# Halves of a tile's product alternate with scores and with the slot steps of the tile before, in the order written for TensorE

## The chip, the cores and the metric

The kernel runs on one NeuronCore of a Trainium2 chip. Five engines work side by side, each in the order of its own queue: PE (TensorE: matmul, with PEld loading its weights), DVE (VectorE), ACT (ScalarE), POOL (GpSimd), and SP, which here only issues DMAs. They wait for one another through semaphores. PE writes to PSUM alone; DVE and ACT read it from there. The metric is the device time of one launch in microseconds, lower is better.

## The reference, cut to what matters

Block-sparse attention is followed by a soft mixture of experts. The attention has 4 batches, 8 heads, 768 positions and 64 elements per head, in blocks of 32 positions. A block of queries sees its own block and both neighbours, the first and the last block, and three sampled blocks; the first and the last query block see everything.

```python
scores = scale * np.matmul(q, k.transpose(0, 1, 3, 2))
scores = np.where(mask, scores, -1000000000.0)
attn = softmax(scores)                       # rows, + 1e-9 below
x = (attn @ v).transpose(0, 2, 1, 3).reshape(3072, 512)

logits = x @ phi                             # 3072 x 32
d = exp(logits - logits.max(0)); d /= d.sum(0) + 1e-9
slot_input = d.T @ x                         # 32 slots of 512
slot_out[e] = np.maximum(slot_input[e] @ w1[e], 0) @ w2[e]   # 8 experts, 4 slots each
c = softmax(logits)                          # over the 32 slots
out = c @ slot_out
```

All of it is float32.

## The kernel before, in words

**Units and tiles.** A batch has 26 units: 4 dense ones (the first and last query block, two head halves r, two of them j) and 22 sparse ones, for 11 pairs of query blocks (g) and two head halves (r = 0, 1). Two pairs make one tile x of 128 rows and 512 columns; pair 0 and the dense units make the tile t = 0, and five further tiles (t = 1 to 5) follow, so 24 tiles in all, 20 of them of four sparse units. Scores of a pair come in one go for r = 0 and r = 1 (L286), so every second period has a group of them. One half of a tile's product, `av_half` (L351), multiplies the probabilities of one r with the values: fixed blocks first (L360), then neighbours and sampled blocks (L378). It accumulates in `avt`, a PSUM buffer of four banks, in the first 65 columns of each. `av_out` (L333) divides by the sums (L336, L337, L339) and writes x. Both halves use the same columns. `av_dense` (L342) does the same for dense units.

**The steps from a tile to slot input**, `moe_front` (L384), in their order: e1 transposes x into PSUM (L392), DVE copies it to xT; e2 multiplies by phi (L437) into columns 128 to 255 of `avt`'s first bank, and ACT copies that to lp; e3 sums the four parts in both layouts (L444, L445), and `top` takes the running maximum (L427, L430); e3b is the exponential dT with its sum, the correction factor, and the copy of the logits to lst, all on ACT (L452 to L457); e4 transposes dT on PE (L461), DVE copies it to d and updates ssum (L465); e5 multiplies d with x (L476), DVE adds it to sacc (L479). The last tile takes other steps for the first three.

**The order.** On PE and DVE the instructions keep the order in which the code emits them; ACT, POOL and SP are ordered by the framework. The main loop goes over periods n, one unit each. A period emits: staging of keys (POOL L194, L199 and ACT L203, five units ahead) and values (POOL L214, two ahead); the scores of unit n + 2 (`do_qk`); what the list X1 holds for n, PE's part; the transpose of unit n's probabilities (`do_tr`, DVE L324); the DVE parts of X1; the row maxima and exponentials of the new unit (`do_soft`, DVE L302, ACT L305); then the list X2, PE's parts and after them DVE's. A step that returns a function leaves its evacuation to that function; e2, e4 and e5 emit theirs at once. `at(n, off, f)` puts f in X1 (even) or X2 (odd) of period n + 1 + off // 2.

Buffers that bear on it: three PSUM tiles for scores (tag s), one shared by e1, e4 and e5 (tag pt), four staged key tiles, eight value tiles, five of transposed probabilities, two of x, one each of xT, lp, dT and d. The framework orders accesses of different engines to `avt`, as to every buffer.

After the last unit come the last tile, the combine weights, and the experts' two products over weights that are partly loaded during the attention.

Of the kernel before, what the change touches and what calls it, by code (L numbers as in the profile page):

```python
# [21 lines left out]
P = 128  # L22
NP = 4
DM = H * D
NS = 32
# [15 lines left out]
KSTEP, VSTEP, EARLY = 5, 2, 4  # L41
KEARLY = 4

EOFF = [2, 3, 5, 6, 7, 8]

CS = 2
CW = DM // CS
# [16 lines left out]
def attn_moe_kernel(ctx, tc, qT, kT, vtab, sampled, phi, w1, w2, out):  # L64
# [224 lines left out]
    def do_soft(u):  # L289
        nm = pw.tile([P, 2], F32, tag="nm", name="nm", bufs=3)  # L290
        if u.dense:
            for n in range(2):
                DVE.tensor_reduce(out=nm[:, n:n + 1], in_=u.s[n], axis=AX.X, op=ALU.max, negate=True)
            nb = pw.tile([P, 1], F32, tag="nb1", name="nb1", bufs=3)
            DVE.tensor_tensor(out=nb, in0=nm[:, 0:1], in1=nm[:, 1:2], op=ALU.min)
            DVE.tensor_scalar(out=nb, in0=nb, scalar1=SCALE, scalar2=None, op0=ALU.mult)  # L296
            u.p = [pw.tile([P, 384], F32, tag="p", name="pd", bufs=PB) for _ in range(2)]
            for n in range(2):
                ACT.activation(out=u.p[n], in_=u.s[n], func=AF.Exp,  # L299
                               bias=nb, scale=SCALE)  # L300
        else:
            DVE.tensor_reduce(out=nm, in_=u.s, axis=AX.X, op=ALU.max, negate=True)  # L302
            u.p = pw.tile([P, 2, 256], F32, tag="p", name="p", bufs=PB)
            for hf in range(2):
                ACT.activation(out=u.p[:, hf, :], in_=u.s[:, hf, :], func=AF.Exp,  # L305
                               bias=nm[:, hf:hf + 1], scale=1.0)
# [8 lines left out]
    def do_tr(u):  # L315
        if u.dense:
            if u.j == 0:
                ptn[0] += 1
            u.pt = ptd[ptn[0] % NPTD]
            for n in range(2):  # L320
                DVE.transpose(out=u.pt[:, 12 * n:12 * n + 12, u.j, :], in_=u.p[n])
        else:
            u.pt = pw.tile([P, 8, 2, BLK], F32, tag="ptt", name="ptt", bufs=PTB)
            DVE.transpose(out=u.pt.rearrange("p k j q -> p j k q"), in_=u.p.rearrange("p j (k q) -> p j k q", k=8))  # L324
# [59 lines left out]
    def moe_front(b, t):  # L384
# [55 lines left out]
            evac(st["lp"], ps, "A")  # L440

        def e3():
            ps = avt[:, 1, 128:2 * P + NS]
            PE.matmul(ps[:, 0:P], lhsT=sel4, rhs=st["lp"], start=True, stop=True)  # L444
            PE.matmul(ps[:, P:P + NS], lhsT=st["lp"], rhs=sel4[:, 0:NS], start=True, stop=True)  # L445
            top(ps, ps[:, P:P + NS])
# [24 lines left out]
                DVE.reciprocal(out=ssum, in_=ssum)  # L471

        def e5():
            ps = psA.tile([P, P], F32, tag="pt", bufs=1, name="ms")
            for c in range(4):
                PE.matmul(ps[32 * c:32 * c + 32, :], lhsT=st["d"], rhs=x[:, c * P:(c + 1) * P],  # L476
                          start=True, stop=True)
            if "al" in st:
                DVE.scalar_tensor_tensor(out=sacc, in0=sacc, scalar=st["al"], in1=ps,  # L479
                                         op0=ALU.mult, op1=ALU.add)  # L480
            else:
                DVE.tensor_copy(out=sacc, in_=ps)
# [13 lines left out]
    def c_soft(g):  # L496
        l = lst[:, 4 * g:4 * g + 4]
        cm = pw.tile([P, 4], F32, tag="cm", name="cm")
        DVE.tensor_reduce(out=cm, in_=l, axis=AX.X, op=ALU.max)
        DVE.tensor_tensor(out=l, in0=l, in1=bc(cm, 4), op=ALU.subtract)  # L500
        ACT.activation(out=l, in_=l, func=AF.Exp)

    def c_norm(g):
        l = lst[:, 4 * g:4 * g + 4]
        cm = pw.tile([P, 4], F32, tag="cm", name="cm")
        DVE.tensor_reduce(out=cm, in_=l, axis=AX.X, op=ALU.add)
        DVE.tensor_scalar(out=cm, in0=cm, scalar1=EPS, scalar2=None, op0=ALU.add)
        DVE.reciprocal(out=cm, in_=cm)
        DVE.tensor_tensor(out=l, in0=l, in1=bc(cm, 4), op=ALU.mult)
# [16 lines left out]
        evac(cT[g], bank, eng)  # L526

    npre = [0]
    X1, X2 = {}, {}
    N = len(units)  # L530
    bytile, both = {}, {}
    qk = [0]
# [21 lines left out]
    def run(d, n):  # L554
        return [f for f in [f() for f in d.pop(n, [])] if f]

    for j, g in enumerate((0, 1, 2, 5)):
        X1.setdefault(N - 12 + 2 * j, []).append(lambda g=g: lambda: c_soft(g))
        X1.setdefault(N - 11 + 2 * j, []).append(lambda g=g: lambda: c_norm(g))

    def at(n, off, f):
        (X1, X2)[off % 2].setdefault(n + 1 + off // 2, []).append(f)

    vn = [0]
    for n in range(-3, N):
        if n >= 0:
            pump_k(n + KSTEP)
        while vn[0] < min(N, n + VSTEP + 1):
            u = units[vn[0]]
            if not u.dense:  # L570
                u.vst = stage_v(u.b, u.i)
            vn[0] += 1
        new = []
        while qk[0] < min(N, n + 3 + (n >= N - EARLY)):
            do_qk(units[qk[0]])
            new.append(units[qk[0]])
            qk[0] += 1
        later = run(X1, n)
        if n >= 0:
            u = units[n]  # L580
            do_tr(u)
        for f in later:
            f()
        for v in new:
            do_soft(v)
        if n >= 0:
            t = None
            if u.dense:
                if u.j == 1:
                    at(n, 0, lambda u=u: av_dense(u))  # L590
                    t = 0 if u.r == 1 else None
            else:
                tt = (u.g + 1) // 2
                bytile.setdefault((u.b, tt, u.r), []).append(u)
                if u.g % 2 == 0:
                    go = lambda b=u.b, t=tt, us=bytile[u.b, tt, u.r], r=u.r: av_half(b, t, us, r)
                    if n == N - 1:
                        last = go
                    elif n == N - 2:
                        at(n, 0, go)  # L600
                    elif u.r == 0:
                        at(n + 1, 0, go)
                    else:
                        at(n, 1, go)
                        t = tt
            if t is not None:
                if t == 0:
                    both[u.b] = both.get(u.b, 0) + 1
                if t > 0 or both[u.b] == 2:
                    fr = {}  # L610
                    for j in range(6):
                        def go(b=u.b, t=t, j=j, fr=fr):
                            if j == 0:
                                fr["f"] = moe_front(b, t)
                            return fr["f"][j]()
                        at(n, EOFF[j], go)
        for f in run(X2, n):
            f()

        while npre[0] < min(NPRE, NPRE * (n - W0) // (N - W1 - W0)):  # L620
            load_w(npre[0], wpre)
            npre[0] += 1
# [3 lines left out]

    rem = []
    for n in range(N, N + 14):
        rem += X1.pop(n, []) + X2.pop(n, [])

    def one():
        if rem:
# [282 lines left out]
```

## Time and profile before

| What | Value |
|---|---|
| median of 3 runs | 608.24 us |
| lowest, highest | 605.45, 613.77 us |
| profiled execution, its own time | 611.44 us |
| its span, first to last instruction | 609.7 us |
| mean granted TensorE clock | 0.636 |
| busy: PE, PEld | 449.6, 270.5 us |
| busy: DVE, ACT, POOL | 254.6, 186.3, 127.3 us |
| the experts' first product starts | 553.1 us |

In the timeline a row begins with its start and its length in us, the engine, the line, the operation, out<-in by the program's names, the shapes and the count of merged instructions; a bracket at the end is the idle time before it and what ended it ("issue": nothing that the profile shows). In the list of waits a row is the waiting engine and line, the releaser, the total in us, the times and the longest. In the rows of windows the columns are the stretch, its length, the busy time and count of PE, PEld, DVE, ACT and POOL, the granted clock, the DMA share and GB/s. The clock row of the page has one digit for each fortieth of the span, in tenths of full speed.

### The profile page before, as it was taken

How to read it: one execution, taken by the hardware profiler on the slowest of the kernel's cores; microseconds unless marked ns; L12 is line 12 of the kernel's file. 1: busy time of each engine (PE TensorE's matmuls, PEld its weight loads, DVE VectorE, ACT ScalarE, POOL GpSimd, SP SyncE). 2: the span in 40 equal slices, each digit the busy share in tenths (PEclk: the TensorE clock that was granted, in tenths of full speed). 3: DMA queues.
4: the chain of work that ended last, by engine and by line, in shares of the span. 5: the costliest groups of instructions: out<-in, count | busy, mean ns of one | idle time of the engine just before them, and what ended most of it. 6: DMA issues, size and time to landing. Idle time of an engine off the chain costs nothing.

```text
span 609.7 us, 28462 instructions
## 1 busy us (share of the span) xinstructions
PE 449.6 (74%) x12629; PEld 270.5 (44%) x12629; DVE 254.6 (42%) x677; ACT 186.3 (31%) x629; POOL 127.3 (21%) x391
## 2 busy tenths in 40 slices
PE   5775477668877676778966776679777765789992
PEld 1353344445355454444454444433545433563551
DVE  3444154335454433443553453354453364523132
ACT  3343144133125224321324341332242342112042
POOL 2421033312221221422101232312112132102000
PEclk9957655665576656555586556665775665557997
DMA  8677600300300003003000003003000021039997
GB/s 306 238 235 267 236 21 19 109 20 12 114 19 26 15 13 122 22 4 121 11 20 21 20 18 110 22 11 105 13 19 13 21 70 47 5 125 400 407 383 242
DMA packets 26510, 60.99 MB, mean 100 GB/s; under 512 B 2705, under 2 KB 15122, under 8 KB 26386
## 3 DMA queue, kind: packets, MB, share of 16 engines
q1 hardware_dynamic: 26386, 59.16, 27.8%
q8 instruction: 99, 1.62, 1.1%
q14 instruction: 25, 0.20, 0.1%
HBM read 52.86 MB, written 6.29 MB: 97 GB/s over the span
## 4 chain that ended last, share of the span: by engine, by line
PE 65%; DVE 13%; issue 12%; ACT 6%; ACTq 2%; DMA 1%; SPq 0%; DVEq 0%
PE avt L378 15%; PE s L286 11%; PE avt L360 10%; PE sd L275 7%; PE avt L347 5%; DVE x L339 3%; PE pf L726 3%; DVE xT L312 3%; PE avt L437 2%; PE pso L734 2%; PE ms L476 2%; PE mxt L392 2%; ACT kst L203 2%; ACT p L305 2%; DVE rs L337 1%
## 5 line engine op out<-in xcount | busy, mean ns | idle before, releaser
L305 ACT ACTIVATE p<-s,nm 128x256 f32<-128x256 f32 x176 | 73.3, 469 | 139.5 <-DVE nm L302 134.4
L214 POOL COPY vrs<-vtile 128x130 f32 x264 | 68.0, 295 | 227.9 <-PE avt L378 203.0
L378 PE MATMUL avt<-vrs,ptt 32*32 32x65 f32 x4224 | 80.0, 289 | 29.9 <-issue 29.9
L286 PE MATMUL s<-kst,qc 64*32 64x256 f32 x1408 | 89.1, 608 | 10.1 <-ACT p L305 7.9
L336 DVE TENSOR_SCALAR rs<-avt 128x4 f32<-128x4 f32 (+1 forms) x56 | 9.0, 161 | 186.5 <-PE avt L378 161.2
L360 PE MATMUL avt<-vtile,ptt 32*64 32x65 f32 x2816 | 61.9, 312 | 31.7 <-DVE x L339 22.7
L378 PEld LDWEIGHTS avt<-vrs,ptt 32*32 32x32 f32 x4224 | 66.9, 129 | 36.9 <-issue 34.5
L199 POOL TENSOR_SCALAR kst<-ktile 128x384 f32<-128x384 f32 x88 | 44.6, 510 | 144.5 <-PE s L286 143.4
L203 ACT ACTIVATE kst<-ktile 128x128 f32 x264 | 63.3, 300 | 36.8 <-PE s L286 23.8
L360 PEld LDWEIGHTS avt<-vtile,ptt 32*64 32x64 f32 x2816 | 51.7, 199 | 49.6 <-DVE x L339 27.3
L302 DVE TENSOR_REDUCE nm<-s 128x2 f32<-128x512 f32 x88 | 59.5, 678 | 30.0 <-PE s L286 29.8
L324 DVE STREAM_TRANSPOSE ptt<-p 128x512 f32<-128x512 f32 x88 | 61.8, 702 | 0.1
L275 PE MATMUL sd<-ktile,qd 64*32 64x384 f32 x256 | 48.1, 826 | 9.5 <-DMA ktile<-in_kT_dram 5.5
L286 PEld LDWEIGHTS s<-kst,qc 64*32 64x32 f32 x1408 | 30.0, 150 | 41.2 <-issue 21.2
L310 ACT COPY lp<-avt 128x128 f32<-128x128 f32 x23 | 6.1, 265 | 135.3 <-PE avt L437 135.3
L347 PE MATMUL avt<-vtile,ptd 32*64 32x65 f32 x1536 | 32.5, 251 | 4.5 <-issue 4.5
L347 PEld LDWEIGHTS avt<-vtile,ptd 32*64 32x64 f32 x1536 | 30.8, 166 | 9.9 <-issue 6.3
L392 PE MATMUL mxt<-ident,x 128*128 128x128 f32 x92 | 28.9, 421 | 7.9 <-DVE x L339 7.9
L437 PE MATMUL avt<-xT,phis 128*32 128x128 f32 x184 | 14.8, 404 | 24.6 <-DVE xT L312 22.8
L299 ACT ACTIVATE pd<-sd,nb 128x384 f32<-128x384 f32 x32 | 16.8, 576 | 45.5 <-DVE nb L296 26.9
L378 PE MATMUL avt<-vtile,ptt 32*32 32x65 f32 x1280 | 24.9, 299 | 2.9 <-issue 2.6
L339 DVE TENSOR_TENSOR x<-avt,rs 128x256 f32<-128x256 f32 (+1 forms) x56 | 23.7, 424 | 1.9
(106 smaller groups left out, 385.5 us busy)
## 6 DMA issues: line engine op xcount, KB each, us to landing
w<-in_w_dram SPq DMA_DIRECT2D x52, 512.0 KB, 9.4
ktile<-in_kT_dram SPq DMA_DIRECT2D x16, 384.0 KB, 5.7
kw<-in_w_dram SPq DMA_DIRECT2D x12, 512.0 KB, 5.6
qc<-in_qT_dram SPq DMA_DIRECT2D x44, 128.0 KB, 2.0
out_dram<-ob SPq DMA_DIRECT2D x20, 256.0 KB, 3.9
vtile<-in_vtab_dram SPq DMA_DIRECT2D x4, 845.0 KB, 5.0
vtile<-in_vtab_dram SPq DMA_DIRECT2D x4, 780.0 KB, 7.3
qd<-in_qT_dram SPq DMA_DIRECT2D x4, 128.0 KB, 2.1
```

The lines of the kernel that those rows point to most:

```text
L199: POOL.tensor_scalar(out=st[:, :, w:w + 96], in0=kv[:, :, (i - 1) * BLK:(i + 2) * BLK], scalar1=SCALE, scalar2=1.0, op0=ALU.mult, op1=ALU. ...
L203: ACT.activation(out=st[:, :, o:o + BLK], in_=kv[:, :, ds(vals[j] * BLK, BLK)], func=AF.Copy, scale=SCALE)
L214: POOL.tensor_copy(out=st[:, j:j + 1, :], in_=vf[:, ds(vals[j], 1), :])
L275: PE.matmul(u.s[n][32 * p:32 * p + 32, :], lhsT=qd[s_, p, u.j, :], rhs=kt[s_, p, 384 * n:384 * (n + 1)], start=True, stop=True)
L286: PE.matmul(u.pair_of[r].s[32 * p:32 * p + 32, j, :], lhsT=q[s_, p, j, :], rhs=kst_[s_, p, :], start=True, stop=True)
L302: DVE.tensor_reduce(out=nm, in_=u.s, axis=AX.X, op=ALU.max, negate=True)
L305: ACT.activation(out=u.p[:, hf, :], in_=u.s[:, hf, :], func=AF.Exp, bias=nm[:, hf:hf + 1], scale=1.0)
L324: DVE.transpose(out=u.pt.rearrange("p k j q -> p j k q"), in_=u.p.rearrange("p j (k q) -> p j k q", k=8))
L339: DVE.tensor_tensor(out=x[lo:hi, r], in0=a[:, :, 0:D], in1=rs[lo:hi].unsqueeze(2).to_broadcast([hi - lo, NP, D]), op=ALU.mult)
L347: PE.matmul(avt[64:128, p, 0:D1], lhsT=u.pt[s_, k].rearrange("p j q -> p (j q)"), rhs=vt[s_, k, u.r, :], start=(k == 0), stop=(k == NB - 1))
L360: PE.matmul(avt[o:o + 64, p, 0:D1], lhsT=u.pt[s_, c].rearrange("p j q -> p (j q)"), rhs=vt[s_, k, r, :], start=(n == 0), stop=False)
L378: PE.matmul(avt[o:o + 32, p, 0:D1], lhsT=u.pt[s_, c, j, :], rhs=v_, start=False, stop=(n == NR))
```

## The change

The two lists become three, addressed by period: X[0] and X[1] are emitted before the scores, X[2] at the end of the period. The first half of a tile's product goes into X[0] of the period after its last unit (before: two periods after), the second half into X[0] of the next one, the dense products into X[0] as well. e1 to e5 get the periods and lists of `EOFF`, counted from the tile's last unit, or of `EOFFL` for the fifth unit from the end. New units with r = 1, whose scores came a period earlier, get their maxima and exponentials before the lists' DVE parts. e3 moves from `avt` to the buffer pt, and e5 from pt to the fourth bank of `avt`.

For a tile whose last unit is n this gives, on PE: period n: first half, then e2 and e3 of the tile before; n + 1: second half, e4 of the tile before, a group of scores; n + 2: e5 of the tile before, e1; n + 3: a group of scores.

```diff
-EOFF = [2, 3, 5, 6, 7, 8]
+EOFF = [(2, 2), (4, 1), (4, 2), (4, 2), (5, 1), (6, 2)]
+EOFFL = [(2, 2), (3, 1), (3, 2), (3, 2), (4, 1), (5, 0)]
...
         def e3():
-            ps = avt[:, 1, 128:2 * P + NS]
+            ps = psA.tile([P, P + NS], F32, tag="pt", bufs=1, name="mlt")
...
         def e5():
-            ps = psA.tile([P, P], F32, tag="pt", bufs=1, name="ms")
+            ps = avt[:, 3, 128:2 * P]
...
-    X1, X2 = {}, {}
+    X = [{}, {}, {}]
...
-    def at(n, off, f):
-        (X1, X2)[off % 2].setdefault(n + 1 + off // 2, []).append(f)
+    def at(n, k, f):
+        X[k].setdefault(n, []).append(f)
...
         new = []
+        later = run(X[0], n) + run(X[1], n)
         while qk[0] < min(N, n + 3 + (n >= N - EARLY)):
             do_qk(units[qk[0]])
             new.append(units[qk[0]])
             qk[0] += 1
-        later = run(X1, n)
         if n >= 0:
             u = units[n]
             do_tr(u)
+        early = [v for v in new if not v.dense and v.r == 1]
+        for v in early:
+            do_soft(v)
         for f in later:
             f()
         for v in new:
-            do_soft(v)
+            if v not in early:
+                do_soft(v)
...
-                    at(n, 0, lambda u=u: av_dense(u))
+                    at(n + 1, 0, lambda u=u: av_dense(u))
...
-                    elif n == N - 2:
-                        at(n, 0, go)
-                    elif u.r == 0:
+                    else:
                         at(n + 1, 0, go)
-                    else:
-                        at(n, 1, go)
-                        t = tt
+                        t = tt if u.r else None
...
-                if t > 0 or both[u.b] == 2:
+                if n < N - 1 and (t > 0 or both[u.b] == 2):
...
-                        at(n, EOFF[j], go)
-        for f in run(X2, n):
+                        d, k = (EOFFL if n == N - 5 else EOFF)[j]
+                        at(n + d, k, go)
+        for f in run(X[2], n):
             f()
...
-        rem += X1.pop(n, []) + X2.pop(n, [])
+        rem += X[0].pop(n, []) + X[1].pop(n, []) + X[2].pop(n, [])
```

More of the change, by code (lines that the diff above doesn't have):

```diff
@@ L557, in attn_moe_kernel @@
     for j, g in enumerate((0, 1, 2, 5)):
-        X1.setdefault(N - 12 + 2 * j, []).append(lambda g=g: lambda: c_soft(g))
-        X1.setdefault(N - 11 + 2 * j, []).append(lambda g=g: lambda: c_norm(g))
-    def at(n, off, f):
-        (X1, X2)[off % 2].setdefault(n + 1 + off // 2, []).append(f)
+        X[1].setdefault(N - 12 + 2 * j, []).append(lambda g=g: lambda: c_soft(g))
+        X[1].setdefault(N - 11 + 2 * j, []).append(lambda g=g: lambda: c_norm(g))
+    def at(n, k, f):
+        X[k].setdefault(n, []).append(f)
     vn = [0]
```

## The prediction, made before the change was run

> **What bounds the kernel now.** I read the page first, then the waits, then the timeline of one tile, engine by engine.
>
> ```profile
> PE 449.6 (74%) x12629; PEld 270.5 (44%) x12629; DVE 254.6 (42%) x677; ACT 186.3 (31%) x629; POOL 127.3 (21%) x391
> PEclk9957655665576656555586556665775665557997
> PE 65%; DVE 13%; issue 12%; ACT 6%; ACTq 2%; DMA 1%; SPq 0%; DVEq 0%
> ```
>
> PE is the bound, but not alone: it is busy 74% of the span, and a quarter of the chain that ended last (13 + 12%) is DVE or PE's own issue. From the third slice to the 35th the clock row reads mostly 5 to 7. The waits name what PE stands for, in us, times and longest:
>
> ```profile
> PE avt L378 <- issue: 32.6, 22, 5.6
> PE avt L437 <- DVE xT L312: 22.8, 23, 1.6
> PE avt L360 <- DVE x L339: 22.7, 23, 1.4
> PE md L461 <- ACT dT L452: 21.0, 15, 2.8
> PE s L286 <- ACT p L305: 7.9, 3, 2.6
> PE mxt L392 <- DVE x L339: 7.9, 20, 0.6
> ACT sp L310 <- DVE sp L312: 7.4, 2, 5.5
> ```
>
> Four of them are one pattern, once per tile: PE issues a step and the next thing in its written order needs the evacuation of that step. One tile of the steady part, PE's rows:
>
> ```profile
> 338.20 0.66 PE L437 MATMUL avt<-xT,phis 128*32 128x128 f32 x8 [0.78 <-DVE xT L312]
> 338.78 1.96 PE L286 MATMUL s<-kst,qc 64*32 64x256 f32 x32
> 340.67 0.80 PE L444 MATMUL avt<-lp,sel 128*128 128x128 f32 x2
> 341.26 0.47 PE L445 MATMUL avt<-sel,lp 128*128 128x32 f32 x2
> 343.03 0.31 PE L461 MATMUL md<-ident,dT 32*128 32x32 f32 x1 [1.30 <-ACT dT L452]
> 343.27 1.96 PE L286 MATMUL s<-kst,qc 64*32 64x256 f32 x32
> 345.16 0.65 PE L476 MATMUL ms<-x,d 128*32 128x128 f32 x8
> 345.75 1.30 PE L360 MATMUL avt<-vtile,ptt 32*64 32x65 f32 x64
> ...
> 349.39 0.91 PE L378 MATMUL avt<-vrs,ptt 32*32 32x65 f32 x40 [0.94 <-issue]
> 351.30 1.30 PE L360 MATMUL avt<-vtile,ptt 32*64 32x65 f32 x64 [1.00 <-DVE x L339]
> ...
> 355.89 0.69 PE L392 MATMUL mxt<-ident,x 128*128 128x128 f32 x2 [0.30 <-DVE x L339]
> 357.36 0.66 PE L437 MATMUL avt<-xT,phis 128*32 128x128 f32 x8 [0.78 <-DVE xT L312]
> ```
>
> From 338.20 to 357.36 a tile takes 19.16 us, of which 1.30 + 0.94 + 1.00 + 0.30 + 0.78 = 4.32 are waits and 14.84 PE's own work. The first half of the tile's product (r0) runs from 345.75 to 350.30, 3.6 us without its 0.94; the second (r1) starts at 351.30 on the same PSUM columns. e1 to e5 are the rows of L392, L437, L444 with L445, L461 and L476, the steps that turn a finished tile x into slot input.
>
> **The change, part by part.** No work is added or removed; in this sum every matmul keeps its price. PE's new order of a tile, read from the lists: r0, e2, e3, r1, e4, scores, e5, e1, scores, where e2 to e5 belong to the tile before, and e1 to this one. The other rows that I need:
>
> ```profile
> 338.96 0.27 ACT L310 COPY lp<-avt 128x128 f32<-128x128 f32 x1 [6.84 <-PE avt L437]
> 341.20 0.71 ACT L203 ACTIVATE kst<-ktile 128x128 f32 x3 [0.44 <-PE s L286]
> 341.81 0.82 ACT L305 ACTIVATE p<-s,nm 128x256 f32<-128x256 f32 x2
> 343.45 0.17 DVE L312 COPY d<-md 128x32 f32<-128x32 f32 x1
> 346.15 0.70 DVE L324 STREAM_TRANSPOSE ptt<-p 128x512 f32<-128x512 f32 x1
> 350.41 0.16 DVE L336 TENSOR_SCALAR rs<-avt 128x4 f32<-128x4 f32 x1 [3.56 <-PE avt L378]
> 350.82 0.42 DVE L339 TENSOR_TENSOR x<-avt,rs 128x256 f32<-128x256 f32 x1
> 351.16 0.68 DVE L302 TENSOR_REDUCE nm<-s 128x2 f32<-128x512 f32 x1
> ```
>
> *r1 no longer follows r0.* r0's normalisation runs from 350.41 to 351.24, 0.83 us, and r1 started 0.06 later. Now e2 (0.66) and e3 (340.67 to 341.73, 1.06) lie between. The buffer named avt has its columns for e2 beside those of r0, and the last wait above (of the experts' part) shows that neighbours in one PSUM buffer are ordered although they share no column, reads included: ACT's copy of one half of sp stood 7.4 us for DVE's copy of the other half. So DVE's normalisation waits for e2 and for lp: about 0.66 + 0.43 later, done 0.66 + 0.43 + 0.83 = 1.92 us after r0. r1 comes 0.66 + 0.43 + 1.06 = 2.15 us after r0. The wait goes: 22.7 us. The cover is 0.2 us thin; without it r1 pays that remainder, not the old 1.00.
>
> The Trainium skill, "PSUM — Partial Sum Buffer", section "PSUM bank collisions raise a hardware error", speaks against putting e2 there: two engines may not access one bank and quadrant together, reads included, so something must order them. The trace agrees with the order (the 7.4 us); by the rule or by the rows the sum is the same only while the 0.2 us hold, and 0.2 x 20 = 4 us worse if they don't (an estimate).
>
> *e1 moves away from r1, e2 away from e1.* e1 now has e4 and 1.96 us of scores behind r1, and the normalisation needs 0.83: the 7.9 us go. e2 has scores and r0 in front, 5 us, where it stood 0.78 us for the xT copy: the 22.8 us go. *e4 behind r1:* dT has r1, 3.6 us like r0, as cover instead of 1.30 us of standing: the 21.0 us go. In all 22.7 + 7.9 + 22.8 + 21.0 = 74.4 us.
>
> *e3 directly behind e2* is the new wait: no scores lie between. From the end of e2 at 338.86: lp starts 0.10 later, takes 0.27, and PE starts 0.06 after what it waits for: 0.43 us. Below that it cannot be; above, if two exponentials stand before lp in ACT's queue, 0.43 + 0.82 = 1.25. I take 0.43, since those exponentials' scores lie a whole r0 earlier: 0.43 x 23 = 9.9 us, at most 29.
>
> *e4's copy d now stands ahead of DVE's transpose of the period.* It waits for e4, thus for r1, and queued behind it are ssum, a transpose, r1's normalisation and the row maximum. From the end of e4: 0.1 to the start of d, which takes 0.17, ssum (one column) about as long, so 0.4; the transpose to 1.1, the normalisation to 2.0 us. PE has 1.9 us of scores; e5, now in avt, must wait for the normalisation's read: 0.1 us, 2 us in 20 tiles. No one else waits: the half that needs the transpose is a period away.
>
> *Scores close to scores.* Between the two groups lie only e5 and e1, 0.65 and two pairs like that at 355.89, together some 1.3, where both halves lay. There are three score tiles, so the second group needs the exponentials of the first one's first unit: maximum at 2.0 to 2.7 us, exponentials to 3.6. PE is there at 1.9 + 0.1 + 0.65 + 1.3 = 3.95. It fits by 0.35. Not if ACT runs both groups of staging copies first (2 x 0.71): then 1.42 - 0.35 = 1.07 us, 21 us in 20 tiles. The second copy starts 0.44 us after what it waits for, and ends before the maximum does, so I take 0. A gain (the 7.9 us of scores behind exponentials) isn't counted either; those are three places around the dense units.
>
> POOL's and SP's transfers keep their periods; value slots come free earlier. The last tiles use a shorter list, and I cost them at nothing: the product tail behind them is unchanged.
>
> *Issue stays.* In this stretch PE stands without a named releaser:
>
> ```profile
> 369.21 0.30 PE L378 MATMUL avt<-vrs,ptt 32*32 32x65 f32 x2 [1.48 <-issue]
> 370.50 1.30 PE L360 MATMUL avt<-vtile,ptt 32*64 32x65 f32 x64 [1.00 <-DVE x L339]
> 371.73 0.52 PE L378 MATMUL avt<-vtile,ptt 32*32 32x65 f32 x32
> 372.06 0.75 PE L378 MATMUL avt<-vrs,ptt 32*32 32x65 f32 x30
> 374.34 1.22 PE L378 MATMUL avt<-vrs,ptt 32*32 32x65 f32 x66 [1.52 <-issue]
> ```
>
> Between the two stops lie 2 + 64 + 32 + 30 = 128 matmuls. That looks like blocks of 128 matmuls with their weight loads, where the next block arrives late: 5.13 us here. One half has 64 + 32 + 30 + 66 = 192 matmuls, so a block that falls inside it still runs out, and one that spans both halves didn't. I keep the 32.6 us.
>
> Sum: the profiled execution took 611.4 us; 611.4 - 74.4 + 9.9 + 2 = 548.9. The median of the runs is 608.2, 0.5% lower, so **546**.
>
> **Rivals.** *The clock rises.* At the granted clock of 1.00 the same steps are shorter:
>
> ```profile
> 316.50:325.50 9.00, 3.97 (x89) 2.20 (x81) 6.52 (x15) 5.46 (x20) 0.99 (x3) 1.00 0.05 15
> 338.20:347.00 8.80, 7.50 (x154) 3.96 (x155) 4.69 (x11) 6.01 (x23) 2.10 (x5) 0.50 0.11 32
> 319.94 1.09 PE L286 MATMUL s<-kst,qc 64*32 64x256 f32 x32
> ```
>
> Scores take 1.09 us instead of 1.96 (the column before the last two is the clock): 1.74 us a tile. The digits of the clock row over the tiles average about 0.6, and (0.6 - 0.5) / 0.5 is a fifth of the time at full clock. If PE without its gaps got it for three fifths: 0.4 x 20 x 1.74 = 14 us, and some 20 with the other steps: 526. For it: r0 after scores and e2 behind are 6 us without a gap. Against: 338.20 to 341.73 was gapless too, at 0.50. Chance 0.22. The Trainium skill, "TensorE: Matmul & The Clock Gate", Part 1, says that the clock is halved by default and freed by one busy window of about 3.4 us; the two values agree with the rows, the gapless 3.5 us at 0.50 only if the window's phase missed them.
>
> *The covers are too thin.* Scores wait 1.07 us (21 us), lp stands behind the exponentials (another 19): 548.9 + 40 = 589, on the median's scale 586. For it: margins of 0.35 and 0.2 us, and ACT's order isn't written by hand. Against: ACT is idle 69% of the span. Chance 0.20.
>
> *Instruction blocks become the bound, and the kernel is slower.* Two halves, two groups of scores of 32 and 25 matmuls in e1 to e5 make 473 a tile, 3.7 blocks. At 5.13 us each it would take 19.0, as long as now: 608, no change, chance 0.07. It decides at 19.16 / 3.7 = 5.2 us; at 5.5, as behind longer transfers (the 5.6 us stop), 20.4 us a tile and 608 + 25 = 633. For it: stops of 32.6 us already. Against: 22 stops, 1.5 us on the average, in 24 tiles, and steps of few matmuls between the halves give a block time to arrive. Chance 0.06. The forecast itself, 536 to 562, has 0.45.
>
> **How the numbers follow.** The range reaches from the clock case to the thin covers: 524 to 590. Outside lie the two cases of the blocks and the edges. Two percent, about what a measurement of this kernel can tell from no change, is 596 to 620: faster 0.45 + 0.22 + 0.20 = 0.87, same 0.07, slower 0.06.
>
> **What would show it.** Right: the waits of L437 on xT, L360 on x, L461 on dT and L392 on x are nearly gone from PE; L444 waits about 0.4 us for lp 23 times; a steady tile takes 16.3 us; issue keeps about 33 us. Wrong: scores (L286) wait for exponentials in every tile, e5 for the normalisation by more than 0.5 us, or r1 still waits for x; a granted clock above 0.70 means that the gain has a second source; issue above 60 us means the blocks.

## The result, and the profile after

The changed kernel takes **538.68 us** (median of four runs, 535.25 to 543.37), the kernel before 608.52 in the same comparison: a ratio of 0.883, with a 95% interval of 0.873 to 0.892. The forecast was 546, in a range of 524 to 590. The profiled execution took 535.25 us, its span is 533.5 us and its mean granted clock 0.734.

The page of the changed kernel, the rows that answer to the first fence of the prediction, with the row of the queue that brings most of the instructions (packets, MB, share of 16 engines):

```profile
PE 416.5 (78%) x12629; PEld 266.3 (50%) x12629; DVE 250.2 (47%) x677; ACT 187.0 (35%) x629; POOL 125.9 (24%) x391
PEclk9957576769577667775687777685877656589996
q8 instruction: 99, 1.62, 1.2%
```

PE does the same 12629 matmuls in 33 us less, and the clock row now reads mostly 5 to 8. Rows of the list of its waits (lines from the change on are two higher than before, further down a few more):

```profile
PE avt L380 <- issue: 44.0, 27, 4.3
PE avt L478 <- DVE x L341: 8.1, 7, 1.6
PE mlt L446 <- ACT lp L312: 7.3, 17, 0.5
PE avt L349 <- DVE sacc L481: 6.6, 3, 2.2
PE avt L362 <- issue: 6.1, 4, 3.7
PE s L288 <- ACT p L307: 4.0, 6, 1.1
PE avt L362 <- DVE ptt L326: 2.7, 7, 0.9
PE avt L349 <- DVE ptd L323: 2.6, 2, 1.3
PE avt L362 <- DVE sacc L481: 2.4, 5, 0.7
PE avt L362 <- DVE x L341: 1.6, 7, 0.2
PE avt L439 <- DVE xT L314: 0.8, 1, 0.8
```

Of the four waits of the kernel before, 74.4 us, r1's for x (L362) has 1.6 us left and e2's for xT (L439) 0.8; e1's for x and e4's for dT are not in the list any more. The largest row is now a stop with no named releaser. A tile of the steady part in the timeline, PE's rows:

```profile
304.51 1.96 PE L288 MATMUL s<-kst,qc 64*32 64x256 f32 x32
306.40 0.65 PE L478 MATMUL avt<-x,d 128*32 128x128 f32 x8
...
312.32 1.04 PE L380 MATMUL avt<-vrs,ptt 32*32 32x65 f32 x80 [0.80 <-issue]
313.28 0.43 PE L439 MATMUL avt<-xT,phis 128*32 128x128 f32 x8
314.15 0.49 PE L446 MATMUL mlt<-lp,sel 128*128 128x128 f32 x2 [0.44 <-ACT lp L312]
...
315.01 1.76 PE L362 MATMUL avt<-vtile,ptt 32*64 32x65 f32 x64 [0.24 <-DVE x L341]
...
319.53 0.52 PE L380 MATMUL avt<-vrs,ptt 32*32 32x65 f32 x28 [1.15 <-issue]
319.99 0.31 PE L463 MATMUL md<-ident,dT 32*128 32x32 f32 x1
320.23 1.96 PE L288 MATMUL s<-kst,qc 64*32 64x256 f32 x32
```

From scores to scores 15.72 us, where the tile of the prediction took 19.16 and the forecast for a steady tile was 16.3. The tiles of the changed kernel differ more than those before: counted from e2 to e2, without the stretches of the dense units and the last tile, they take 12.9 to 19.8 us, before 18.6 to 22.4.

The balance, from the page (busy) and from the whole list of PE's waits (rows with "issue" as stops, all others as named waits; some 12 us of gaps too short for the list are in neither):

| PE, us | before | after | difference |
|---|---|---|---|
| busy, the same matmuls | 449.6 | 416.5 | -33.1 |
| named waits | 101.6 | 46.7 | -54.9 |
| stops without a named cause | 46.7 | 57.3 | +10.6 |
| gaps in neither | 11.8 | 13.0 | +1.2 |
| span | 609.7 | 533.5 | -76.2 |

So three questions went to the chip: which part of the change removes which wait, where the 33 us of shorter matmuls come from, and what the stops are. My theory was that the waits' removal pays twice, once itself and once by the clock, and that the stops are blocks of 128 matmuls that arrive late, together with their weight loads. The rivals: one single piece of the change brings it all; the clock rises for another reason than the closed gaps; the stops belong to places in the work.

All runs in one table. The medians of before were 608.8, 611.3 and 610.2 us in the three comparisons that the other rows come from; ratios are to these. The last four columns are of the one profiled execution. r0_early has no interval, since three of its four runs, the profiled one among them, lie 1.6 to 1.9% above its fastest.

| Kernel | median, us | ratio, 95% interval | named waits | stops | PE busy | clock |
|---|---|---|---|---|---|---|
| before | 608.5 | | 101.6 | 46.7 | 449.6 | 0.636 |
| r0_early | 585.1 | 0.96, no interval | 89.4 | 36.1 | 446.1 | 0.664 |
| e2_near | 565.6 | 0.924 (0.920 to 0.929) | 66.1 | 50.6 | 440.9 | 0.661 |
| together | 562.9 | 0.924 (0.917 to 0.930) | 71.7 | 48.1 | 430.1 | 0.701 |
| r0_early_pt | 552.4 | 0.905 (0.898 to 0.912) | 63.6 | 45.0 | 431.8 | 0.693 |
| opt | 549.3 | 0.900 (0.896 to 0.904) | 52.2 | 49.5 | 434.0 | 0.706 |
| split_r0 | 544.2 | 0.893 (0.887 to 0.899) | 58.2 | 44.9 | 423.6 | 0.730 |
| shift | 540.2 | one run | 43.3 | 55.0 | 427.6 | 0.728 |
| after | 538.7 | 0.883 (0.873 to 0.892) | 46.7 | 57.3 | 416.5 | 0.734 |
| tr_first | 534.6 | 0.880 (0.875 to 0.884) | 46.8 | 62.2 | 402.2 | 0.774 |
| opt3 | 526.8 | 0.864 (0.859 to 0.870) | 49.6 | 44.9 | 418.5 | 0.706 |
| fill | 613.1 | 1.006 (1.002 to 1.010) | 68.3 | 52.7 | 481.1 | 0.658 |
| fill2 | 614.8 | 1.007 (1.004 to 1.011) | 64.9 | 59.9 | 475.4 | 0.713 |

### The profile page after: what moved, and what is told of

Same layout as the page of the kernel before. It is cut to its first block, busy times and chain, and to the rows that moved or that the text cites. A ratio compares the mean times of both kernels' runs of the same rounds, so it can differ in the third digit from the quotient of the medians.

```text
span 533.5 us, 28450 instructions
## 1 busy us (share of the span) xinstructions
PE 416.5 (78%) x12629; PEld 266.3 (50%) x12629; DVE 250.2 (47%) x677; ACT 187.0 (35%) x629; POOL 125.9 (24%) x391
## 4 chain that ended last, share of the span: by engine, by line
PE 61%; DVE 13%; issue 13%; DMA 5%; ACT 4%; ACTq 1%; SPq 0%; DVEq 0%
PE avt L380 15%; PE s L288 11%; PE avt L362 10%; PE avt L349 7%; PE sd L277 7%; DMA w<-in_w_dram 4%; DVE nm L304 3%; PE pf L730 3%; DVE ptt L326 2%; PE mlt L446 2%; DVE ptd L323 2%; PE avt L439 2%; ACT p L307 2%; PE mxt L394 2%; DVE x L341 1%
## 5 line engine op out<-in xcount | busy, mean ns | idle before, releaser
L380 PE MATMUL avt<-vrs,ptt 32*32 32x65 f32 x4224 | 75.8, 271 | 43.7 <-issue 43.6
L380 PEld LDWEIGHTS avt<-vrs,ptt 32*32 32x32 f32 x4224 | 63.5, 122 | 48.5 <-issue 46.6
L288 PE MATMUL s<-kst,qc 64*32 64x256 f32 x1408 | 81.0, 511 | 7.4 <-ACT p L307 4.0
L362 PE MATMUL avt<-vtile,ptt 32*64 32x65 f32 x2816 | 59.9, 278 | 13.2 <-issue 6.1
L362 PEld LDWEIGHTS avt<-vtile,ptt 32*64 32x64 f32 x2816 | 49.1, 171 | 34.4 <-issue 10.7
L338 DVE TENSOR_SCALAR rs<-avt 128x4 f32<-128x4 f32 (+1 forms) x56 | 8.4, 150 | 90.5 <-ACT lp L312 59.0
L314 DVE COPY d<-md 128x32 f32<-128x32 f32 x23 | 4.4, 191 | 97.2 <-PE md L463 97.2
L288 PEld LDWEIGHTS s<-kst,qc 64*32 64x32 f32 x1408 | 30.0, 132 | 36.7 <-issue 17.9
L349 PE MATMUL avt<-vtile,ptd 32*64 32x65 f32 x1536 | 37.9, 279 | 11.8 <-DVE sacc L481 6.6
L277 PE MATMUL sd<-ktile,qd 64*32 64x384 f32 x256 | 41.7, 734 | 5.9 <-DMA ktile<-in_kT_dram 5.2
L349 PEld LDWEIGHTS avt<-vtile,ptd 32*64 32x64 f32 x1536 | 36.4, 192 | 14.9 <-DVE sacc L481 7.4
L301 ACT ACTIVATE pd<-sd,nb 128x384 f32<-128x384 f32 x32 | 16.8, 576 | 52.8 <-DVE nb L298 50.6
L295 DVE TENSOR_REDUCE nm<-sd 128x1 f32<-128x384 f32 x32 | 17.1, 548 | 16.8 <-PE sd L277 16.7
L394 PE MATMUL mxt<-ident,x 128*128 128x128 f32 x92 | 23.2, 401 | 0.0
L380 PE MATMUL avt<-vtile,ptt 32*32 32x65 f32 x1280 | 22.4, 269 | 0.4 <-issue 0.4
```

Of the source, the lines that this page charges most:

```text
L277: PE.matmul(u.s[n][32 * p:32 * p + 32, :], lhsT=qd[s_, p, u.j, :], rhs=kt[s_, p, 384 * n:384 * (n + 1)], start=True, stop=True)
L288: PE.matmul(u.pair_of[r].s[32 * p:32 * p + 32, j, :], lhsT=q[s_, p, j, :], rhs=kst_[s_, p, :], start=True, stop=True)
L349: PE.matmul(avt[64:128, p, 0:D1], lhsT=u.pt[s_, k].rearrange("p j q -> p (j q)"), rhs=vt[s_, k, u.r, :], start=(k == 0), stop=(k == NB - 1))
L362: PE.matmul(avt[o:o + 64, p, 0:D1], lhsT=u.pt[s_, c].rearrange("p j q -> p (j q)"), rhs=vt[s_, k, r, :], start=(n == 0), stop=False)
L380: PE.matmul(avt[o:o + 32, p, 0:D1], lhsT=u.pt[s_, c, j, :], rhs=v_, start=False, stop=(n == NR))
L394: PE.transpose(ps[:, c, :], x[:, c * P:(c + 1) * P], ident)
```

## The experiments

### Parts of the change, one at a time

**r0_early**: the kernel before with the first half of a product one period earlier, so that it no longer stands directly ahead of the second.

```diff
-                        at(n + 1, 0, go)
+                        at(n, 0, go)
```

> The kernel before, with the first half of each product one period earlier and nothing else; e3 stays in avt. Theory (accesses to one buffer are ordered even between different columns): r1 no longer waits for x (22.7 us gone) and e4 no longer for dT (21.0 us gone), but r0 now writes the bank that e3b still reads and waits in their place for the copy of lst, about 1.5 us in 20 tiles, 31 us: net 13 us, 595 us. Rival (only shared columns matter): no such wait, 565 us or less.

Measured: 585.1 us, the four runs between 575 and 586, 10 below the theory's 595. Rows of the waits of r0_early:

```profile
PE avt L360 <- ACT lst L457: 27.3, 17, 1.8
PE avt L437 <- DVE xT L312: 22.8, 23, 1.7
PE mxt L392 <- DVE x L339: 9.9, 20, 0.7
```

Separating the halves takes away r1's wait for x and e4's for dT (together 43.7 us), and a new one of 27.3 takes most of it back: a half waits until ACT has copied the logits to lst. e3 still writes the buffer avt there, beside the columns of the halves. This is the ordering of neighbours in one PSUM buffer, on which the prediction counted for e2, at its full price. The named waits fall by 12.2 us, as the theory said (13); the rest of the gain is mostly stops, which fall by 10.6 and of which it said nothing.

**r0_early_pt**: the same, and e3 writes the buffer pt, as in the change.

```diff
-            ps = avt[:, 1, 128:2 * P + NS]
+            ps = psA.tile([P, P + NS], F32, tag="pt", bufs=1, name="mlt")
```

> The same, with e3 moved from avt to the buffer pt as in the change. Theory: both waits go and nothing takes their place, 608 - 44 = 565 us; with the clock's share (the changed kernel's PE is busy 33 us less, with 74 us of waits removed) about 20 us more, 545 us. Rival (the spread of e1 to e5 is what counts): little gain, 590 us or more.

Measured: 552.4 us, between the theory's 565 without the clock's share and 545 with it. Rows of the waits of r0_early_pt:

```profile
PE avt L437 <- DVE xT L312: 22.7, 23, 1.6
PE mxt L392 <- DVE x L339: 10.7, 20, 0.7
```

The wait for lst is gone, the other two stand much as before (22.7 and 10.7). These two edits, one step in time and one other buffer, bring 56 of the 70 us (608.8 to 552.4); the rest of the change brings the rest, which no run here splits up further.

**together**: the changed kernel with the two halves directly behind one another again.

```diff
+                    if u.r == 0 and n < N - 2:
+                        go = lambda go=go: go()()
...
-                        at(n + 1, 0, go)
+                        at(n + (2 if u.r == 0 and n < N - 2 else 1), 0, go)
```

> The changed kernel, with the first half moved back to stand directly before the second. Theory: r1 waits 1.0 us for x again in 20 tiles, and with the gap some full clock is lost: 538.7 + 20 = 559, to 568 us with the clock. Rival (the clock alone made the gain): the clock falls little and the time stays under 545 us.

Measured: 562.9 us, as expected. Rows of the waits of together:

```profile
PE avt L362 <- DVE x L341: 22.9, 23, 1.2
PE mlt L446 <- ACT lp L312: 16.2, 17, 1.6
```

r1's old wait is back (22.9, and 22.7 in the kernel before), and e3's for lp doubles. Named waits rise by 25.0 us over the changed kernel, the stops fall by 9.2, and the same matmuls take 13.6 us longer.

**e2_near**: the changed kernel with e2 brought back near e1, so that the xT copy has little in front; e1 and e5 move one list ahead with it.

```diff
-EOFF = [(2, 2), (4, 1), (4, 2), (4, 2), (5, 1), (6, 2)]
+EOFF = [(2, 1), (2, 2), (4, 2), (4, 2), (5, 1), (6, 1)]
```

> The changed kernel, with e2 back directly behind e1 (e5 ahead of both). Theory: e2 waits 0.8 us for xT again, e3 no longer 0.44 us for lp (r0 lies between): 0.35 us in 20 tiles, 7 us, and a little clock: 546 to 552 us. Rival (e2's place has no price of its own): 536 to 541 us.

Measured: 565.6 us, 14 above the upper end. Rows of the waits of e2_near:

```profile
PE avt L439 <- DVE xT L314: 31.1, 20, 2.5
PE avt L478 <- DVE x L341: 13.9, 8, 2.7
```

The wait for xT is larger than it ever was: 1.26 us in a usual tile, where the timeline has a row maximum of DVE between e1 and the copy (0.78 in the kernel before). Against the changed kernel named waits rise by 19.4 us, the stops fall by 6.7, and the matmuls take 24.4 more: the profiled span is 35.9 us longer (569.4 against 533.5). This execution was the slowest of the four, with a clock of 0.661 where the other three had 0.693 to 0.696; by the medians the loss is 27 us, some 1.4 us for each microsecond of waiting.

### The clock

**fill**: the kernel before with products that nothing reads in three of the four gaps.

```diff
+    def idle_work(cols):
+        ps = psA.tile([P, P], F32, tag="pt", bufs=1, name="idle")
+        for c in cols:
+            PE.matmul(ps[:, 0:c], lhsT=ident, rhs=ident[:, 0:c], start=True, stop=True)
...
+        if r == 1 and t > 0:
+            idle_work((P, 16))
```

> The kernel before, with matmuls whose result nobody reads on PE in the three places of a tile where it stands (between e1 and e2, between e3 and e4, between the halves), each about as long as the wait; the computation is unchanged. Theory (gapless PE work raises the granted clock, and a higher clock alone saves time): the waits keep their ends, the clock goes from 0.64 to 0.70 or more, the steps between shorten, 580 to 595 us. Rival (the clock only follows the shorter time, or saves nothing): 608 to 615 us.

Measured: 613.1 us, the rival's time. It did not settle the point, since its products were too short: in most tiles 0.3 to 0.6 us of each gap remained, and the clock rose to 0.658 only.

**fill2**: the same, filled further.

```diff
-            idle_work((P, 16))
+            idle_work((P, P, 32))
...
-            idle_work((P, NS))
+            idle_work((P, P, 16))
```

> The kernel before, with more of the matmuls that nobody reads, so that the three places of a tile are filled to the end at half clock (the first filling left 0.3 to 0.6 us in each). Theory (gapless PE work raises the clock, and the clock saves time): the share of the tile part at full clock goes from 17% to 35% or more, the granted clock to 0.70 or more, and the time to 585 us (27 us of clock less some 5 us of overfilling). Rival (filling changes the clock little; the clock rises because matmuls are less waited for): 613 to 620 us.

Measured: 614.8 us at a clock of 0.713 (0.689 to 0.721 in its ten runs, 0.626 to 0.664 in those of the kernel before beside it). The clock is the theory's, the time, 30 us above the theory's 585, the rival's. The groups of fill2 that are filling (busy, mean ns, idle before):

```profile
L354 PE MATMUL idle<-ident 128*128 128x128 f32 (+1 forms) x240 | 44.5, 334 | 3.6 <-DVE nm L302 1.8 <-issue 1.3 <-DVE sacc L491 0.5
L445 PE MATMUL avt<-ident 128*128 128x96 f32 x76 | 19.1, 407 | 0.0
```

Of 475.4 us busy 63.6 is filling; the kernel's own matmuls take 411.8, 37.8 less than before in the same order. So filled gaps alone raise the clock and shorten the work, as much as the change did (33.1). Not all gaps closed: e4 still waits 18.6 us for dT (21.0 before), since the six products ahead of it take 1.46 us at a clock of 0.50, as planned, but 0.82 at 1.00. The time does not fall, because 63.6 us of filling and 13.2 of further stops stand against 36.7 us of waits and the 37.8. The clock is worth having, but not at the price of filling.

### The stops

**shift**: the changed kernel with 32 small products that nothing reads ahead of the loop. PE executes each as two matmuls (12693 in its profile against 12629), so all later work lies 64 matmuls later in the program.

```diff
+    for _ in range(SHIFT):
+        PE.matmul(avt[:, 0, 0:8], lhsT=ident, rhs=ident[:, 0:8], start=True, stop=True)
```

> The changed kernel with 32 small products that nothing reads ahead of the loop, 64 records of TensorE. Theory of instruction blocks: the stops without a named cause stay 128 matmul records apart and come at the same count from the program's start, so that each lies 64 records earlier in the work than in the changed kernel, in the middle between two of its stops. Rival: the stops belong to places in the work (a buffer, a semaphore that the profile does not show), and stay in front of the same products, 64 records later by count. The time changes by less than 2% in either case.

Measured: 540.2 us, 0.3% above the changed kernel. Two stops of the changed kernel, in the timeline:

```profile
60.13 1.00 PE L362 MATMUL avt<-vtile,ptt 32*64 32x65 f32 x38 [3.67 <-issue]
...
444.33 0.33 PE L380 MATMUL avt<-vrs,ptt 32*32 32x65 f32 x11 [3.35 <-issue]
444.59 0.65 PE L439 MATMUL avt<-xT,phis 128*32 128x128 f32 x8
```

and the stops of shift at the same counts:

```profile
60.17 0.39 PE L381 MATMUL avt<-vrs,ptt 32*32 32x65 f32 x26 [2.57 <-issue]
...
447.38 1.35 PE L381 MATMUL avt<-vrs,ptt 32*32 32x65 f32 x75 [2.46 <-issue]
448.66 0.65 PE L440 MATMUL avt<-xT,phis 128*32 128x128 f32 x8
```

The second stop of the pair came with 11 products left before e2 and comes with 75 left, 64 earlier in the work. Counted over the matmul records of the traces, the stopped matmul has the same number in both kernels:

```
matmuls ahead of the stopped one (and the rest of a division by 128)
after   986 (90)  1114 (90)  2389 (85)  ...  9150 (62)  11446 (54)  12085 (53)
shift   986 (90)  1114 (90)  2389 (85)  ...  9150 (62)  11446 (54)  12085 (53)
```

The other stops have the same rests within two or three. In every kernel here the distance from one stop to the next is a multiple of 128, less 0 to 5; I take the small drift for PE's instructions of other kinds, which the count leaves out. The stops belong to the program's position, not to the work. The theory of blocks stands, and the trace shows the blocks themselves: the queue q8 above brings 99 packets, and 12629 / 128 = 98.7. fill2 has 12945 matmuls, and the row of its page follows (12945 / 128 = 101.1):

```profile
q8 instruction: 101, 1.65, 1.1%
```

A packet of 16 KB brings 128 matmuls and their weight loads. In the records of the changed kernel each of the 36 stops over 0.25 us ends 1.24 to 1.59 us after such a packet has landed, its transfer takes 0.88 to 1.48 us, and it starts 1.14 us (median) after the first matmul of the previous block. Two of these packets never start less than 3.26 us apart. At the stops of 3.67 and 4.3 us, in the stretch of large transfers at the beginning (the DMA engines are busy 70% of the first 80 us), the packet started 5.6 and 4.4 us after the first matmul of the previous block; that the large transfers hold it up is not shown by a run.

The Trainium skill, "Runtime: NRT & Kernel Launch", section "Instruction fetch mechanics", says that an engine gets its instructions in blocks of 16 KiB, 256 instructions, by a queue of its own; the trace agrees in both numbers. It also says that PE holds 2048 instructions, eight such blocks, and that the fetch is hidden behind the issue. That does not fit: PE stands 36.1 (r0_early) to 62.2 us (tr_first) for it, and at the stops the block that is missing was asked for only when the one ahead of it had begun.

**split_r0**: the changed kernel with the second 16 of the scores ahead of r0 moved into the middle of r0, so that a block takes longer to run out.

```diff
-    def do_qk(u):
+    def do_qk(u, js=(0, 1)):
...
+            if n == 1 and mid is not None:
+                mid()
...
+                do_qk(v, (0,))
+                hold[n + 1] = [v]
```

> The changed kernel, with the second 16 matmuls of the group of scores ahead of r0 moved into the middle of r0, in 16 tiles. Theory (PE's instructions come in blocks of 128 matmuls with their weight loads, 3.2 us apart at the least, so a stretch of 128 quick matmuls stands): stops inside r0 nearly vanish, the sum of PE's waits named issue falls from 57 us to 40 or less, 515 to 525 us. Rival (the stops come from something else in the products, their data or their buffers): issue stays at 50 us or more, 535 to 542 us.

Measured: 544.2 us. The stops fall from 57.3 to 44.9 us. Rows of the waits of split_r0:

```profile
PE mlt L449 <- ACT lp L313: 10.7, 17, 1.3
PE avt L363 <- DVE ptt L327: 8.9, 18, 0.9
```

Named waits rise by 11.5, since some covers became too thin, and busy time by 7.1: the time does not fall, and my expectation is missed by 20 us. The theory had the stops inside r0 nearly vanish, and that failed too: counted in the traces, they fall from 24.5 to 20.1 us only. Those inside r1, whose order is unchanged, fall as much, from 25.7 to 20.1, and in shift, where nothing but the position differs, to 19.7. So a part of the 12.4 us is where the blocks happen to end, and this run does not show that a longer way through r0 removes its stops.

### Other orders

**tr_first**: the changed kernel with DVE's transpose of the period emitted ahead of the lists, and so ahead of the copy d that waits for e4.

```diff
+        if n >= 0:
+            do_tr(units[n])
         while qk[0] < min(N, n + 3 + (n >= N - EARLY)):
...
-            do_tr(u)
```

> The changed kernel with one edit: in a period, the steps of VectorE that follow the transpose of the tile one period back (the read of the transposed tile and the maximum) are given out ahead of the lists' work of the period instead of behind it. Nothing on TensorE changes its place. In the changed kernel TensorE waits 8.1 us (7 times, 1.6 us with the rows shown; 8.1 in all) for the step at L341 in front of the last of the slot input parts (e5). If that wait comes from VectorE's order alone, it falls under 2 us, nothing else appears, and the time is 529 to 534 us (538.7 less 5 to 9). The rival: VectorE has the same work in the same stretch, so that the wait moves to another of its products (the sum in front of the dense scores or the normalised tile), and the time stays at 537 to 541 us.

The edit moves the transpose of the probabilities; the expectation speaks of other steps of DVE. Measured: 534.6 us (526.0 to 539.7); the interval of its ratio overlaps that of the changed kernel. Rows of the waits of tr_first:

```profile
PE avt L349 <- DVE ptd L323: 6.8, 5, 1.7
PE avt L362 <- DVE ptt L326: 4.1, 10, 0.9
PE avt L478 <- DVE x L341: 3.1, 5, 1.6
```

e5's wait falls from 8.1 to 3.1 us, and the transposed probabilities take the 5 us back (ptd from 2.6 to 6.8, ptt from 2.7 to 4.1). The rival was right on the waits; the order of DVE is no gain that these runs can tell. The profiled execution is the fastest of its six (526.0 us), so its clock and busy time stand better in the table than the median does.

**opt**: split_r0, and in r1's period e3 in the middle of r1, e2 in the buffer pt, and the normalisation ahead of the transpose.

```diff
-EOFF = [(2, 2), (4, 1), (4, 2), (4, 2), (5, 1), (6, 2)]
+EOFF = [(2, 2), (4, 1), (5, 1), (5, 1), (5, 1), (6, 2)]
...
-            ps = avt[:, 0, 128:2 * P]
+            ps = psA.tile([P, P], F32, tag="pt", bufs=1, name="mlp")
```

> The same, and e3 moved into the middle of r1 with e2 in pt, and in the period of r1 DVE's normalisation ahead of its transpose. Theory: blocks in r1 get 1 us more too, the waits of e3 for lp (7 us) and most of those of e5 for x (8 us) go, r1 waits 0.35 us for x (7 us): issue 30 us or less, 500 to 515 us. Rival (as above): 530 us or more.

Measured: 549.3 us, far from the expectation. Rows of the waits of opt:

```profile
PE avt L363 <- issue: 12.6, 10, 4.8
PE avt L363 <- DVE x L342: 7.7, 15, 0.7
PE avt L363 <- DVE ptt L327: 6.4, 16, 0.9
```

e3's wait for lp is nearly gone (0.4 us), r1's for x is back (7.7), and the stops now fall at the beginning of halves as well. The matmuls take 10 us longer than in split_r0; why, I did not find out.

**opt3**: the changed kernel in the order r0, e2, scores, first half of r1, e3, second half of r1, e4, scores, e5, e1, with e2 in pt.

```diff
-EOFF = [(2, 2), (4, 1), (4, 2), (4, 2), (5, 1), (6, 2)]
+EOFF = [(3, 2), (4, 1), (5, 2), (5, 3), (5, 3), (7, 2)]
...
-                        at(n + 1, 0, go)
+                        at(n + 1, 2 * u.r, go)
```

> The changed kernel in another order of the same products: r0, e2, scores A, first half of r1, e3, second half of r1, e4, scores B, e5, e1; e2 and e3 write the bank of the slot products and not the bank behind r1. Each product that TensorE waits for has at least 2.5 us of other products ahead of it. Theory of covers: the 46.7 us of named waits of the changed kernel fall to 30 or less, and the time to 510 to 525 us. Rival: what is left is set by the stops without a named cause (57.3 us in the changed kernel) and by the granted clock, which no order of the products touches: named waits fall and the time stays at 535 us or above.

Measured: **526.8 us**, the fastest kernel here; its interval lies below those of the changed kernel and of tr_first. Rows of the waits of opt3:

```profile
PE avt L382 <- issue: 26.1, 22, 2.6
PE avt L362 <- DVE sacc L483: 10.7, 12, 1.8
PE md L465 <- ACT lst L461: 7.7, 5, 2.3
```

Neither theory had it right. The wait for lp is gone, those for x nearly, but named waits did not fall (49.6 against 46.7), since r0 now waits for the addition behind e5, in its own buffer, and e4 for lst. What fell are the stops, by 12.4 us, though the rival held that no order touches them. Inside the second halves, which e3 now splits, they fall from 25.7 to 8.8 us, far more than a shift of position did (19.7); inside the first halves from 24.5 to 20.3; elsewhere they rise from 7.2 to 15.7. That fits blocks that last longer where other steps lie within the run of short products, but no run takes that one piece out of opt3. In the profiled execution its granted clock (0.706) is lower than the changed kernel's at nearly the same busy time; the mean clock over the span does not give the busy time by itself, and I leave that open.

## Why the prediction was right, and where not

The time was right (538.7, forecast 546), the list of waits nearly so, and two terms that the sum set at zero were not zero; they have opposite signs.

**r1 no longer follows r0, e1, e2 and e4 have cover: right.** Of 74.4 us 72.0 are gone (1.6 and 0.8 left). *r0_early* and *together* show the first of them from both sides.

**The normalisation waits for e2 and lp, by the order within a PSUM buffer: right.** The first step of the normalisation in the list of groups of the changed kernel (busy, mean ns, idle before, and what ended it; the idle time holds more than this order, since DVE may have nothing to do):

```profile
L338 DVE TENSOR_SCALAR rs<-avt 128x4 f32<-128x4 f32 (+1 forms) x56 | 8.4, 150 | 90.5 <-ACT lp L312 59.0 <-PE avt L349 21.7 <-PE avt L380 9.8
```

In the tile above lp's copy ends at 314.10, L338 starts at 314.13, the normalisation ends at 314.96 and r1 starts at 315.01. The cover of 0.2 us was as thin as said: r1 waits for x in seven tiles, 0.2 us each, 1.6 in all where the estimate was 4. The rule of the Trainium skill, "PSUM — Partial Sum Buffer", section "PSUM bank collisions raise a hardware error", that was weighed there, agrees: L338 reads columns that lp's copy does not touch, and stands for it; in r0_early the same order between lst and a half costs 27.3 us. The row that the prediction took the order from, ACT's 7.4 us for DVE's copy of sp, could not carry it. In the timeline of the kernel before:

```profile
579.84 0.29 DVE L312 COPY sp<-pso 128x128 f32<-128x128 f32 x1 [5.89 <-PE pso L734]
580.22 0.27 ACT L310 COPY sp<-pso 128x128 f32<-128x128 f32 x1 [5.52 <-DVE sp L312]
```

The two copies write one tile as well as read one buffer, and ACT starts 0.38 us after DVE, which had itself stood 5.89 us for PE: of the 5.52 us nearly all would have passed without the order.

**e3 directly behind e2: right.** 0.44 us in the tile above, 0.43 forecast; 7.3 us (17 times) against 9.9.

**e5 behind the normalisation: mechanism right, size off.** Forecast 0.1 us in 20 tiles, 2 us; measured 8.1 in seven. The sum covered the DVE chain of 2.0 us with scores of 1.9 us, their length at the clock of 0.50. In three of the seven places, 3.6 of the 8.1 us, the scores ahead took 1.09 us, and the chain is as long as ever. Of the other four, two come behind the scores of dense units, one behind scores of 1.96 us and one behind no scores at all. One of the three in the timeline of the changed kernel:

```profile
374.41 1.09 PE L288 MATMUL s<-kst,qc 64*32 64x256 f32 x32
...
376.69 0.43 PE L478 MATMUL avt<-x,d 128*32 128x128 f32 x8 [1.19 <-DVE x L341]
```

A cover made of matmuls shrinks when the clock rises.

"No one else waits" stood beside it, and that was wrong. e5 now writes the buffer of the halves, and the products that follow it there stand for DVE's addition to sacc, which reads e5's result: 6.6 us in L349 and 2.4 in L362, two rows that the kernel before does not have. It is the order within a PSUM buffer once more, which the prediction priced for e2 and not for e5. Another 2.7 and 2.6 us are waits for transposed probabilities (ptt, ptd).

**Scores close to scores: right.** They wait 4.0 us for exponentials (7.9 before).

**"I keep the 32.6 us" of stops: wrong.** That row is 44.0 us now, all stops together 57.3 against 46.7. While the named waits fell by 54.9 us, the stops rose by 10.6. That waits give the next block time to arrive fits *together* and *e2_near*, which have 25.0 and 19.4 us more waits than the changed kernel and 9.2 and 6.7 us fewer stops. It is not the whole: r0_early has fewer waits than the kernel before and fewer stops too, and tr_first, with PE's order unchanged and matmuls 14.3 us shorter, has 4.9 us more stops than the changed kernel, as if shorter matmuls used up a block sooner. How the 10.6 divide is open. The observation of 128 matmuls was right, and the rivals made of it too extreme: they took the 5.13 us of one pair of stops for every block, while the smallest distance of two blocks is 3.26 us, some 12 us for the 3.7 blocks of a tile. By that estimate it decides inside a half, not over a tile.

**"Every matmul keeps its price": wrong, and the largest miss.** The granted clock rose to 0.734, above the 0.70 that was named as the sign of a second source, and the same matmuls took 33.1 us less. The scores in the list of groups of the kernel before (busy, mean ns, idle before):

```profile
L286 PE MATMUL s<-kst,qc 64*32 64x256 f32 x1408 | 89.1, 608 | 10.1 <-ACT p L305 7.9 <-ACT pd L299 2.2
```

and of the changed kernel:

```profile
L288 PE MATMUL s<-kst,qc 64*32 64x256 f32 x1408 | 81.0, 511 | 7.4 <-ACT p L307 4.0 <-issue 2.3 <-ACT pd L301 0.9
```

The mean moved because more groups met the full clock, not because a group got another price. Of the groups of 32 scores without a gap, 37 ran at a clock of 0.50 to 0.52 in the kernel before and 2 at 0.98 to 1.00, in the changed kernel 17 and 10, with 8 between; the median lengths are 1.96 us and 1.09 us in both.

So the rival with the clock, given 0.22 and some 20 us, happened together with the forecast rather than instead of it. *fill2* shows that filled gaps raise it. *e2_near*, nearly the changed order but with gaps, had 0.661 to 0.696 in its four runs, the changed kernel 0.725 to 0.746; *together*, with 0.701 to 0.733, overlaps with that and decides nothing.

The span fell by 76.2 us, the sum had 62.5 (74.4 - 9.9 - 2). The 13.7 between them are 33.1 of shorter matmuls, less 10.6 of stops, less 7.6 by which the named waits fell short (54.9 against 62.5), less 1.2 of short gaps. The forecast met the time partly because its misses lie on both sides, and that part was luck.

## What to carry to other kernels

When waits on TensorE are closed, count three terms and not one: the wait itself, the clock that follows (here 0.6 us of shorter matmuls for each microsecond of named waits, 0.25 to 0.86 in the other kernels with the same matmuls), and the instruction blocks, whose stops can grow when waits and matmuls get shorter (here by 10.6 us; no fixed rate came out). Cover a chain on another engine by matmuls at their length at full clock. Long runs of short matmuls can use up a block of 128 faster than the next one arrives; opt3, which puts other steps between and into them, has 12.4 us fewer stops than the changed kernel and is the fastest, while split_r0, with the same idea and the same fall, gained no time. And give steps that meet in time separate PSUM buffers.

## What the runs showed of the hardware that was not expected

The packets of instructions, each with 128 matmuls and their weight loads, start no closer than 3.26 us in these traces, and where PE stands the next is asked for only about 1.1 us (median) after the previous one has begun to run, up to 5.6 us in the changed kernel. The stops come to 36 to 62 us in all of these kernels, and lie 64 matmuls earlier in the work when 64 matmuls are put ahead of it.

Matmuls that nothing reads raise the clock too (0.636 to 0.713 in fill2) and make the kernel's own 8% shorter in busy time (449.6 to 411.8), yet leave the total where it was.
